# Output projection of a recurrent attention kernel: early weight chunks in 512-column matmuls, the last five in halves

## The chip, the cores and the metric

The kernel runs on one core of one Trainium2 chip (trn2). The metric is the time of one execution on the device in microseconds (us). The kernel before took 1822.86 us, the median of three runs (1820.21, 1822.86 and 1832.62).

A core has five engines that matter here. TensorE does matmuls (PE in the profile, its weight loads are PEld), VectorE (DVE) and ScalarE (ACT) do elementwise work, GpSimd (POOL) and SyncE (SP) mostly issue DMAs. TensorE writes to PSUM, an accumulator memory with banks of 512 float32 columns by 128 partitions; the engines work from SBUF. The engines run side by side and wait for one another by semaphores; on each engine the instructions run in their order.

## The reference, cut to what matters

The output joins two independent parts along the last axis. Part A is a convolution by FFT with gates and is not touched by the change. Part B is a recurrent attention: 64 segments of 32 tokens, each of them with 8 memory rows in front that the segment before has made.

```python
mem = mem0
for s in range(n_seg):                                # 64 segments
    h = concat([mem, x[:, s*32:(s+1)*32]], axis=1)    # 40 rows of 1024
    q, k, v = h @ Wq, h @ Wk, h @ Wv                  # 32 heads of 128 each
    p = softmax(where(mask, q @ k.T * scale, -1e9))
    o = p @ v
    o = einsum('bhte,hed->btd', o, Wo)                # output projection, 4096 -> 1024
    mem = o[:, :8]
    outs.append(o[:, 8:])
```

Segment s+1 needs the memory rows of segment s, so the segments follow one another strictly. Each needs all four weight matrices (Wq, Wk, Wv and Wo, 8 MB each in bfloat16), and they don't all fit into SBUF.

## The kernel before, in words

The program has a front part (part A, and the parts of the keys, queries and values that depend only on x) and then a loop over the 64 segments, unrolled. In the loop the order of the instructions is the order of the program (`manual_schedule`, line 896): each engine gets its instructions as they are written.

The weights are cut into 64 **chunks** of 128 by 2048 elements (512 KB): 16 each of Wk, Wq, Wv and Wo. A chunk of Wo is one pair of heads, `hp` 0 to 15. Most chunks stay in SBUF. Sixteen are "streamed" (`STREAM`, line 29): SP loads them anew in every segment from DRAM into a ring of five buffers (`fetch`, L722 and L720; tiles `wring`). A buffer comes free when the matmuls of its chunk are done (`done`, line 860), and `done` starts the next load. Two of the streamed chunks of Wo, 13 (KEPT_A) and 9 (KEPT_B), are loaded once only, in segment 0. From then on they lie as raw bits in spare columns of PSUM: quarters 0 to 3 of each. From segment 1 on, VectorE copies one quarter at a time into an SBUF tile (`quarter` and `quarter_b`, all through L795) before TensorE uses it. These copies borrow SBUF buffers by their tags ("E", "rot", "QT"), and each has to wait until the earlier content of that buffer has been used.

A segment runs so: keys and queries of two head groups (`Proj`, L938, with accumulators `acc`), transposes, scores, softmax, values, `attend` and `evac_o` (L1007 to L1019), and then the output projection into `yacc`. The projection turns the attention output `OT` (two groups, OT0 and OT1) into 40 rows of 1024. Columns 0 to 511 of the result stand in PSUM partitions 0 to 63 and columns 512 to 1023 in partitions 64 to 127, so each step is a **pair** of matmuls (dh = 0 and 1) that write the two halves of the partitions. `project` (line 1022) does the two pairs of one head, each 256 columns wide: half f = 0 goes into the bank `yacc[0]`, half f = 1 into the bank `yacc[1]`. `out_half` does a chunk's two heads for one half. The order of the chunks is FIRST (0, 1, 2, 3), then 4, then group 1's attention (attend, evac_o, on line 1089), then 5, 6, 7, some quarters, 8, and LAST (10, 15, 11, 12, 14). FIRST and LAST go through the chunks twice, first all halves f = 0 and then all halves f = 1; the others do both halves of a chunk together. In LAST the remaining quarters are put in between (`steps`).

When half f = 0 is complete, ScalarE copies it to the tile Y (L1118). While TensorE does half f = 1, `fill_mem` (L885 on TensorE, L892 on VectorE) turns the memory rows of Y's first half into the operand hT of the next segment. The next segment's first matmuls (keys, k0, four chunks that need only this half) then start while ScalarE copies the second half of Y. After them `fill_mem` handles that second half.

The accumulators `acc` and `yacc` share one pool of two PSUM banks (`ps_acc`, line 780, tag "acc"), eight tiles a segment: k0, q0, k1, q1, pv0, pv1, yacc[0], yacc[1]. A new tile waits until all readers of the bank's earlier tile are done.

Of the kernel before, what the change touches and what calls it, by code (L numbers as in the profile page):

```python
# [10 lines left out]
F32 = mybir.dt.float32  # L11
I32 = mybir.dt.int32
ACT = mybir.ActivationFunctionType
ALU = mybir.AluOpType
# [4 lines left out]
NEG = -1.0e9  # L19


FIRST, LAST = (0, 1, 2, 3), (10, 15, 11, 12, 14)
KEPT_A, KEPT_B = (3, 13, 0), (3, 9, 0)
PART = (3, 4, 0)
O_ORDER = (*FIRST, 4, 5, 6, 7, 9, 13, 8, *LAST)
ORDER = [(0, kc, 0) for kc in (0, 1, 4, 5)] + [(1, kc, 0) for kc in (0, 1)] + [(0, kc, 0) for kc in (2, 3, 6, 7)] + \
    [(1, kc, 0) for kc in range(2, 8)] + [(m, kc, 1) for m in (0, 1) for kc in range(8)] + \
    [(2, kc, g) for g in range(2) for kc in range(8)] + [(3, hp, 0) for hp in O_ORDER]
STREAM = (0, 6, 13, 19, 24, 29, 35, 40, 45, 51, 52, 54, 56, 57, 58, 63)
# [391 lines left out]
def b_kernel(ctx: ExitStack, tc, x, mem0, Wq, Wk, Wv, Wo, outb, n_seg, run_a):  # L421
    nc = tc.nc
# [314 lines left out]
    with c0p:  # L737
# [16 lines left out]
        for g in range(2):  # L754
# [23 lines left out]
    one = ctx.enter_context(tc.tile_pool(name="b_one", bufs=1, side="right", reuse_waits="tile"))  # L778
# [15 lines left out]
    def bits(dst, src):  # L794
        nc.vector.tensor_scalar(out=dst, in0=src, scalar1=0, scalar2=None, op0=ALU.bitwise_or)  # L795

    def like(ap, home):
        return ap.rearrange("p (b x) -> p b x", b=4) if len(home.shape) == 3 else ap

    def quarter_b(q, tag):  # L800
        t = one.tile([128, 256], I32, tag=tag, name="quarter_b")
        w = []
        for home, at in B_homes[q]:
            n = home.shape[1] * (home.shape[2] if len(home.shape) == 3 else 1)
            if home.shape == B_rest[:].shape:
                part = home.bitcast(BF)
            else:
# [32 lines left out]
    def quarter(q, tag):  # L840
        t = one.tile([128, 512], BF, tag=tag, name="quarter")
        bits(t[:].bitcast(I32), OTi[:, q, 160:416])
        return [(o, o + 256, t[:, 256 * dh:256 * dh + 256]) for dh, o in enumerate(quarter_cols(q))]

    def pieces(ch):
        if ch in res:
            return [(0, 2048, res[ch])]
        if now[0] == 0 and ch in at_hand:
            return [(0, 2048, at_hand[ch][0])]
        if ch == PART:  # L850
            return [(0, 512, part[:]), (512, 2048, live[now[0], ch][1][:, 512:2048])]
        return [(0, 2048, live[now[0], ch][1][:])]

    def columns(ps, a, b):
        for lo, hi, w in ps:
            x, y = max(a, lo), min(b, hi)
            if x < y:
                yield x, y, w[:, x - lo:y - lo]

    def done(ch):  # L860
        if now[0] == 0 and ch in at_hand:
            place_late(1, at_hand[ch][1])
        elif ch in streamed and (now[0] == 0 or ch not in kept):
# [32 lines left out]
    with tc.manual_schedule():  # L896
        for _ in range(RING - 2):
            fetch()
        load_x(0)
        Y = one.tile([128, 512], BF, tag="PT", name="Y0")  # L900
        nc.vector.memset(Y[:], 0.0)
        for dh in range(2):
            nc.gpsimd.dma_start(Y[64 * dh:64 * dh + NM, :], mem0[:, dh * 512:(dh + 1) * 512])
        nc.tensor.matmul(SB[:, 0:320], lhsT=ident[:], rhs=P_pad[:].rearrange("p b k -> p (b k)"), start=True, stop=True,
                         skip_group_check=True)
# [7 lines left out]
        for s in range(n_seg):  # L913
# [105 lines left out]
                nc.scalar.copy(OT[:], o_view)  # L1019
                return OT  # L1020

            def project(h, f, w, OT, stop=False):
                k = 40 * (h % 16)
                m = min(64, 640 - k)
                lhsT = OT[:].rearrange("p c i q -> p (c i q)")[:, k:k + m]
                for dh in range(2):
                    o = (h % 2) * 1024 + dh * 512 + f * 256
                    for x, y, r in columns(w, o, o + 256):
                        nc.tensor.matmul(yacc[f][64 * dh:64 * dh + m, x - o:y - o], lhsT=lhsT,  # L1029
                                         rhs=r, start=(h == (0, 2 * FIRST[-1])[f] and x == o), stop=stop,  # L1030
                                         tile_position=(0, 64 * dh))

            def out_half(hp, f, OT, stop=False):
                w = pieces((3, hp, 0))
                for hh in range(2):
                    project(2 * hp + hh, f, w, OT, stop and hh == 1)
                if f == 1:
                    done((3, hp, 0))

            def out_proj(hps, OT):  # L1040
                for hp in hps:
                    for f in range(2):
                        out_half(hp, f, OT)

            def out_quarter(ch, q, w):
                project(2 * ch[1] + q // 2, q % 2, w, OT1)

            if s == 0:
                fill_mem(hT, Y, 0)
            k0 = Proj(0, 0).run(4)  # L1050
# [27 lines left out]
            OT0 = evac_o(0)  # L1078
# [3 lines left out]
                load_x(s + 1)  # L1082
            V1 = pv1.evac()
            yacc = [ps_acc.tile([128, 512], F32, tag="acc", name="yacc") for f in range(2)]
            for f, hps in enumerate((FIRST, FIRST[-1:] + FIRST[:-1])):
                for hp in hps:
                    out_half(hp, f, OT0)
            out_proj((4,), OT0)
            attend(1, PT1, V1)
            OT1 = evac_o(1)  # L1090
            qs = {}
            if s == 0:
                out_proj((5, 6, 7), OT0)
                out_proj((9, 13, 8), OT1)
                steps = {}
            else:
                qs["B", 0], qs["A", 0] = quarter_b(0, "E"), quarter(0, "rot")
                out_proj((5, 6, 7), OT0)
                qs["B", 2] = quarter_b(2, "QT")
                out_quarter(KEPT_B, 0, qs["B", 0])  # L1100
                qs["A", 2] = quarter(2, "E")
                out_quarter(KEPT_A, 0, qs["A", 0])
                qs["A", 1] = quarter(1, "rot")
                out_proj((8,), OT1)
                steps = {(0, 0): [("B", 2), ("B", 1, "QT")], (0, 1): [("A", 2), ("A", 3, "E")],
                         (0, 3): [("A", 1), ("B", 3, "rot")], (1, 0): [("B", 1)], (1, 1): [("A", 3)], (1, 2): [("B", 3)]}
            Y = one.tile([128, 512], BF, tag="PT", name="Y")
            for f, hps in enumerate((LAST, LAST[-1:] + LAST[:-1])):
                for n, hp in enumerate(hps):
                    if f == 1 and n == 3 and not last:  # L1110
                        fill_mem(pend[s + 1][0], Y, 0)
                    out_half(hp, f, OT1, n == 4)
                    for step in steps.get((f, n), ()):
                        if len(step) == 2:
                            out_quarter(KEPT_A if step[0] == "A" else KEPT_B, step[1], qs.pop(step))
                        else:
                            qs[step[:2]] = (quarter if step[0] == "A" else quarter_b)(*step[1:])
                nc.scalar.copy(Y[:, 256 * f:256 * f + 256], yacc[f][:, 0:256])  # L1118
            for dh in range(2):
                nc.gpsimd.dma_start(bass.AP(outb.tensor, outb.offset + SEG * s * 2048 + 512 * dh, [[2048, 32], [1, 512]]),  # L1120
                                    Y[64 * dh + NM:64 * dh + 40, :])
# [71 lines left out]
```

## Time and profile before

| what | value |
|---|---|
| runs, median (lowest to highest) | 1822.86 us (1820.21 to 1832.62) |
| span of the profiled execution, first to last instruction | 1811.8 us |
| the profiled execution's own time | not listed apart from the runs; the median less the span is 11.1 us |
| PE busy | 1701.8 us (94%), 30996 matmuls |
| DVE, ACT, POOL busy | 1010.3, 680.7, 266.7 us (56%, 38%, 15%) |
| second-half copies of Y, start of the first and the last | 475.2 and 1807.5 us |
| the same as time of one segment, mean of 63 | 21.15 us |
| matmuls and weight loads of one segment (1555.54 to 1576.38 us) | 461 and 459 |
| DMA share in the loop | 0.97 to 0.98 in stretches of 100 us from 1000 to 1700 us |

The page of the profile gives busy times and shares of the whole span. The timeline lists instructions in order of time: start, duration, engine, line, operation, output<-inputs, shape and how many were merged into the row, and in brackets the idle time of the engine before it and what ended it. Matmuls are pipelined, so a row's duration overlaps the next row; the distance from start to start is what counts. L1029 is the projection, L938 the keys, queries and values.

### The profile page before, as it was taken

Reading aid. Unit: us, or ns where it says so; the run is one execution under the profiler, and the core shown is the slowest. Engines: PE = TensorE matmul, PEld = TensorE weight load, DVE = VectorE, ACT = ScalarE, POOL = GpSimd, SP = SyncE. Lnnn points to the kernel's source line nnn. Section 1 sums busy time; section 2 is a strip of 40 time slices with the busy share of each in tenths; the row PEclk is TensorE's granted clock in tenths of the full one; section 3 lists DMA queues with packets and bytes.
Section 4 is the critical chain, followed back from the end, with each engine's and each line's share of the span. In section 5 each row is a group of like instructions: output and inputs, shape, how many; then the busy total and the mean of one; then the engine's idle time right before and its main releaser. Section 6 shows DMA issues by size and latency. Waiting matters only on the chain.

```text
span 1811.8 us, 71373 instructions
## 1 busy us (share of the span) xinstructions
PE 1701.8 (94%) x30996; PEld 1000.8 (55%) x31028; DVE 1010.3 (56%) x3391; ACT 680.7 (38%) x1195; POOL 266.7 (15%) x499
## 2 busy tenths in 40 slices
PE   6888996759899999999999999999999999999998
PEld 3443322324566666666666666666666666666665
DVE  9927874201455555555555555555555555555555
ACT  6955651112233333333333333333333333333333
POOL 4003341100111111111111111111111111111111
PEclk9999999889999999999999999999999999999999
DMA  9989889997999999999999999999999999999998
GB/s 340 370 305 305 311 258 320 306 335 210 344 365 361 357 350 360 358 363 353 361 356 358 357 352 360 370 358 360 361 355 362 356 358 366 367 363 356 357 358 300
DMA packets 233070, 623.34 MB, mean 344 GB/s; under 512 B 72802, under 2 KB 72946, under 8 KB 232756
## 3 DMA queue, kind: packets, MB, share of 16 engines
q1 hardware_dynamic: 160948, 550.58, 82.4%
q0 software_dynamic: 17056, 45.13, 7.1%
q10 hardware_dynamic: 54752, 23.07, 4.7%
q8 instruction: 243, 3.98, 0.9%
q14 instruction: 71, 0.58, 0.1%
HBM read 563.63 MB, written 57.67 MB: 343 GB/s over the span
## 4 chain that ended last, share of the span: by engine, by line
PE 77%; DMA 9%; DVE 6%; ACT 4%; issue 3%; ACTq 0%; POOL 0%; SPq 0%; another core or an unknown queue 0%; POOLq 0%; DVEq 0%
PE acc L938 33%; PE yacc L1029 24%; PE kb_ps L622 5%; DMA wring<-WS 4%; PE tps L885 3%; PE tps L957 2%; PE vb_ps L763 2%; ACT OT L1019 2%; DMA REC<-stage 2%; DVE mx L972 1%; DVE E L974 1%; ACT s_sb L247 1%; PE OTp L1007 1%; PE s_ps L245 1%; PE SB L963 1%
## 5 line engine op out<-in xcount | busy, mean ns | idle before, releaser
L1029 PEld LDWEIGHTS <-OT 128*64 128x64 bf16 x8255 | 439.1, 109 | 54.6 <-ACT OT L1019 36.9
L938 PEld LDWEIGHTS <-rec 128*32 128x32 bf16 x12288 | 289.4, 96 | 269.3 <-DVE rec L892 35.2
L947 ACT CAST qkv_sb<-acc 128x512 bf16<-128x512 f32 x384 | 225.1, 586 | 352.2 <-PE acc L938 346.9
L938 PE MATMUL acc<-Wres,rec 128*32 128x512 bf16 x3328 | 240.2, 382 | 2.0 <-issue 1.8
L938 PE MATMUL acc<-wring,rec 128*32 128x512 bf16 x2300 | 229.0, 382 | 8.5 <-DMA wring<-WS 7.3
L1029 PE MATMUL yacc<-Wmore,OT 128*64 128x256 bf16 (+1 forms) x2560 | 220.7, 274 | 0.0
L938 PE MATMUL acc<-Wmid,rec 128*32 128x512 bf16 x3072 | 212.1, 379 | 0.5 <-issue 0.3
L1029 PE MATMUL yacc<-wring,OT 128*64 128x256 bf16 x2448 | 194.9, 273 | 2.7 <-DMA wring<-WS 2.5
L1118 ACT CAST Y<-yacc 128x256 bf16<-128x256 f32 x128 | 47.7, 373 | 269.8 <-DVE quarter_b L795 170.8
L938 PE MATMUL acc<-pw,rec 128*32 128x512 bf16 x1796 | 144.7, 380 | 2.0 <-issue 1.9
L795 DVE TENSOR_SCALAR quarter<-OTp 128x256 int32<-128x256 int32 x252 | 99.9, 418 | 74.3 <-ACT OT L1019 74.3
L1019 ACT CAST OT<-OTp 128x640 bf16<-128x640 f32 x128 | 87.4, 683 | 138.5 <-PE OTp L1011 138.5
L1120 POOL DMA_DIRECT2D out_dram<-Y x128 | 63.9, 503 | 496.3 <-ACT Y L1118 496.0
L892 DVE COPY rec<-tps 128x32 bf16<-128x32 bf16 x128 | 22.4, 175 | 193.6 <-PE tps L885 193.6
L938 PE MATMUL acc<-Wlate,rec 128*32 128x512 bf16 x1536 | 117.3, 379 | 0.1
L1057 DVE COPY KT<-tps 128x512 bf16<-128x512 bf16 x64 | 27.2, 425 | 150.8 <-PE tps L885 150.8
L972 DVE TENSOR_REDUCE mx<-SB 128x8 f32<-128x320 f32 x128 | 63.0, 492 | 78.4 <-PE SB L966 78.4
L880 POOL DMA_DIRECT2D rec<-REC x64 | 36.4, 568 | 453.4 <-PE acc L938 437.9
L977 ACT ACTIVATE E<-E 128x320 f32<-128x320 f32 x128 | 60.1, 469 | 78.3 <-DVE E L974 78.3
L1029 PE MATMUL yacc<-Wlate,OT 128*64 128x256 bf16 x1024 | 79.2, 276 | 6.0 <-issue 0.2
L622 PE MATMUL kb_ps<-XBT,pw 128*128 128x512 bf16 x313 | 81.1, 397 | 2.6 <-DMA pw<-in_B_Wk_dram 1.2
L922 POOL COPY KT<-rec 128x128 bf16<-128x128 bf16 x128 | 38.5, 301 | 253.3 <-PE SB L966 253.3
(224 smaller groups left out, 2627.4 us busy)
## 6 DMA issues: line engine op xcount, KB each, us to landing
wring<-WS SPq DMA_DIRECT2D x831, 512.0 KB, 6.0
wring<-WS SPq DMA_DIRECT2D x64, 384.0 KB, 5.4
rec<-REC POOLq DMA_DIRECT2D x64, 192.0 KB, 5.6
SK<-s_sb SPq DMA_DIRECT2D x16, 512.0 KB, 5.3
SU<-s_sb SPq DMA_DIRECT2D x16, 512.0 KB, 5.6
Kg<-SK SPq DMA_DIRECT2D x32, 256.0 KB, 4.1
Ug<-SU SPq DMA_DIRECT2D x32, 256.0 KB, 5.5
REC<-stage ACTq DMA_DIRECT2D x16, 512.0 KB, 12.9
```

The costliest lines, as they stand in the source:

```text
L622: nc.tensor.matmul(ps[:], lhsT=ws[kc][:, hl * 128:(hl + 1) * 128], rhs=xbt(kc).rearrange("p s t -> p (s t)"), start=(kc == 0), stop=(kc == 7))
L795: nc.vector.tensor_scalar(out=dst, in0=src, scalar1=0, scalar2=None, op0=ALU.bitwise_or)
L885: nc.tensor.matmul(dst[e:e + 32, :], lhsT=src[:, e:e + 32], rhs=ident[:], start=True, stop=True, is_transpose=True, tile_position=(0, e))
L922: nc.gpsimd.tensor_copy(KT[:, :, :, 32:40], KBs[:, 128 * g:128 * g + 128].rearrange("p (c i t) -> p i c t", c=4, i=4))
L938: nc.tensor.matmul(self.acc[32 * c:32 * c + 32, :], lhsT=hT[:, ch[1], :], rhs=w[:, 512 * c:512 * c + 512], start=(ch == chs[0]), stop=(ch ...
L947: nc.scalar.copy(sb[:], self.acc[:])
L972: nc.vector.tensor_reduce(out=mx[:], in_=S, op=ALU.max, axis=AX.X)
L977: nc.scalar.activation(E[:], E[:], ACT.Exp, scale=scale)
L1019: nc.scalar.copy(OT[:], o_view)
L1029: nc.tensor.matmul(yacc[f][64 * dh:64 * dh + m, x - o:y - o], lhsT=lhsT, rhs=r, start=(h == (0, 2 * FIRST[-1])[f] and x == o), stop=stop, ...
L1118: nc.scalar.copy(Y[:, 256 * f:256 * f + 256], yacc[f][:, 0:256])
L1120: nc.gpsimd.dma_start(bass.AP(outb.tensor, outb.offset + SEG * s * 2048 + 512 * dh, [[2048, 32], [1, 512]]), Y[64 * dh + NM:64 * dh + 40, :])
```

## The change

Instead of two banks by half, most of the projection goes into one bank. `project` takes a range of columns and a bank. The chunks EARLY (0 to 4), 5, 6, 7 and 8 (in segment 0 also 9 and 13) are done by `out_full`: one matmul of 512 columns in place of two of 256, all into `yacc[0]`. Only LAST stays in halves. Its half f = 0 is accumulated in the other bank, `yacc[1]`, together with quarters 2 of the kept chunks. For that half, ScalarE copies the sum of the early chunks, columns 0 to 255 of `yacc[0]`, to a float32 tile y0; after half f = 0, VectorE adds y0 and the bank `yacc[1]` into Y, where ScalarE made a copy before. Half f = 1 of LAST goes on in `yacc[0]`, columns 256 to 511, and ScalarE copies it to Y as before. Since y0 takes the buffer "rot", the copies and uses of quarters 1, 2 and 3 change their places.

```diff
-FIRST, LAST = (0, 1, 2, 3), (10, 15, 11, 12, 14)
+EARLY, LAST = (0, 1, 2, 3, 4), (10, 15, 11, 12, 14)
...
-            def project(h, f, w, OT, stop=False):
+            def project(h, a, b, w, OT, bank, at, start=False, stop=False):
...
-                    o = (h % 2) * 1024 + dh * 512 + f * 256
-                    for x, y, r in columns(w, o, o + 256):
-                        nc.tensor.matmul(yacc[f][64 * dh:64 * dh + m, x - o:y - o], lhsT=lhsT,
-                                         rhs=r, start=(h == (0, 2 * FIRST[-1])[f] and x == o), stop=stop,
+                    o = (h % 2) * 1024 + dh * 512 + a
+                    for x, y, r in columns(w, o, o + b - a):
+                        nc.tensor.matmul(bank[64 * dh:64 * dh + m, at + x - o:at + y - o], lhsT=lhsT, rhs=r,
+                                         start=start and x == o, stop=stop, skip_group_check=True,
                                          tile_position=(0, 64 * dh))
...
+            def out_full(hps, OT):
+                for hp in hps:
+                    w = pieces((3, hp, 0))
+                    for hh in range(2):
+                        project(2 * hp + hh, 0, 512, w, OT, yacc[0], 0, start=hp == 0 and hh == 0)
+                    done((3, hp, 0))
+            def out_half(hp, f, first, stop):
+                w = pieces((3, hp, 0))
+                for hh in range(2):
+                    project(2 * hp + hh, 256 * f, 256 * f + 256, w, OT1, yacc[1 - f], 256 * f,
+                            start=first and f == 0 and hh == 0, stop=stop and hh == 1)
+                if f == 1:
+                    done((3, hp, 0))
...
+            def out_quarter(ch, q, in_last=False):
+                f = q % 2
+                project(2 * ch[1] + q // 2, 256 * f, 256 * f + 256, qs.pop((ch, q)), OT1,
+                        yacc[1] if in_last and f == 0 else yacc[0], 256 * f)
+            def bring(ch, q, tag):
+                qs[ch, q] = (quarter if ch == KEPT_A else quarter_b)(q, tag)
...
-                steps = {(0, 0): [("B", 2), ("B", 1, "QT")], (0, 1): [("A", 2), ("A", 3, "E")],
-                         (0, 3): [("A", 1), ("B", 3, "rot")], (1, 0): [("B", 1)], (1, 1): [("A", 3)], (1, 2): [("B", 3)]}
+                bring(KEPT_B, 0, "E")
+                bring(KEPT_A, 0, "rot")
+                out_full((5, 6, 7), OT0)
+                bring(KEPT_B, 2, "QT")
+                out_quarter(KEPT_B, 0)
+                bring(KEPT_A, 2, "E")
+                out_quarter(KEPT_A, 0)
+                out_full((8,), OT1)
+                steps = {(0, 1): [(KEPT_B, 2), (KEPT_B, 1, "QT")], (0, 3): [(KEPT_A, 2)],
+                         (1, 0): [(KEPT_A, 1, "E"), (KEPT_B, 1), (KEPT_B, 3, "rot"), (KEPT_A, 3, "QT")],
+                         (1, 2): [(KEPT_A, 1)], (1, 3): [(KEPT_B, 3), (KEPT_A, 3)]}
             Y = one.tile([128, 512], BF, tag="PT", name="Y")
+            y0 = one.tile([128, 256], F32, tag="rot", name="y0")
+            nc.scalar.copy(y0[:], yacc[0][:, 0:256])
...
-                nc.scalar.copy(Y[:, 256 * f:256 * f + 256], yacc[f][:, 0:256])
+                if f == 0:
+                    nc.vector.tensor_tensor(out=Y[:, 0:256], in0=yacc[1][:, 0:256], in1=y0[:], op=ALU.add)
+                else:
+                    nc.scalar.copy(Y[:, 256:512], yacc[0][:, 256:512])
```

In `steps` a key (f, n) says after which chunk of LAST something happens; an entry with a tag is a copy by VectorE (`bring`), one without is a use by TensorE (`out_quarter`). `pieces`, `columns`, `done`, `quarter` and `quarter_b` are unchanged.

More of the change, by code (lines that the diff above doesn't have):

```diff
@@ L19 @@
 NEG = -1.0e9
-FIRST, LAST = (0, 1, 2, 3), (10, 15, 11, 12, 14)
+EARLY, LAST = (0, 1, 2, 3, 4), (10, 15, 11, 12, 14)
 KEPT_A, KEPT_B = (3, 13, 0), (3, 9, 0)
 PART = (3, 4, 0)
-O_ORDER = (*FIRST, 4, 5, 6, 7, 9, 13, 8, *LAST)
+O_ORDER = (*EARLY, 5, 6, 7, 9, 13, 8, *LAST)
 ORDER = [(0, kc, 0) for kc in (0, 1, 4, 5)] + [(1, kc, 0) for kc in (0, 1)] + [(0, kc, 0) for kc in (2, 3, 6, 7)] + \
@@ L1026, in project @@
                 for dh in range(2):
-                    o = (h % 2) * 1024 + dh * 512 + f * 256
-                    for x, y, r in columns(w, o, o + 256):
-                        nc.tensor.matmul(yacc[f][64 * dh:64 * dh + m, x - o:y - o], lhsT=lhsT,
-                                         rhs=r, start=(h == (0, 2 * FIRST[-1])[f] and x == o), stop=stop,
+                    o = (h % 2) * 1024 + dh * 512 + a
+                    for x, y, r in columns(w, o, o + b - a):
+                        nc.tensor.matmul(bank[64 * dh:64 * dh + m, at + x - o:at + y - o], lhsT=lhsT, rhs=r,
+                                         start=start and x == o, stop=stop, skip_group_check=True,
                                          tile_position=(0, 64 * dh))
-            def out_half(hp, f, OT, stop=False):
+            def out_full(hps, OT):
[5 more added lines that the diff above has]
+            def out_half(hp, f, first, stop):
                 w = pieces((3, hp, 0))
                 for hh in range(2):
-                    project(2 * hp + hh, f, w, OT, stop and hh == 1)
+                    project(2 * hp + hh, 256 * f, 256 * f + 256, w, OT1, yacc[1 - f], 256 * f,
+                            start=first and f == 0 and hh == 0, stop=stop and hh == 1)
                 if f == 1:
                     done((3, hp, 0))
[L1040 to L1046, printed above, removed]
+            def out_quarter(ch, q, in_last=False):
[4 more added lines that the diff above has]
+                qs[ch, q] = (quarter if ch == KEPT_A else quarter_b)(q, tag)
             if s == 0:
@@ L1084, in b_kernel @@
             yacc = [ps_acc.tile([128, 512], F32, tag="acc", name="yacc") for f in range(2)]
[L1085 to L1088, printed above, removed]
+            qs = {}
+            out_full(EARLY, OT0)
             attend(1, PT1, V1)
             OT1 = evac_o(1)
-            qs = {}
             if s == 0:
-                out_proj((5, 6, 7), OT0)
-                out_proj((9, 13, 8), OT1)
+                out_full((5, 6, 7), OT0)
+                out_full((9, 13, 8), OT1)
                 steps = {}
             else:
[L1097 to L1104, printed above, removed]
-                steps = {(0, 0): [("B", 2), ("B", 1, "QT")], (0, 1): [("A", 2), ("A", 3, "E")],
-                         (0, 3): [("A", 1), ("B", 3, "rot")], (1, 0): [("B", 1)], (1, 1): [("A", 3)], (1, 2): [("B", 3)]}
+                bring(KEPT_B, 0, "E")
+                bring(KEPT_A, 0, "rot")
+                out_full((5, 6, 7), OT0)
+                bring(KEPT_B, 2, "QT")
[6 more added lines that the diff above has]
+                         (1, 2): [(KEPT_A, 1)], (1, 3): [(KEPT_B, 3), (KEPT_A, 3)]}
             Y = one.tile([128, 512], BF, tag="PT", name="Y")
+            y0 = one.tile([128, 256], F32, tag="rot", name="y0")
+            nc.scalar.copy(y0[:], yacc[0][:, 0:256])
             for f, hps in enumerate((LAST, LAST[-1:] + LAST[:-1])):
@@ L1111, in b_kernel @@
                         fill_mem(pend[s + 1][0], Y, 0)
-                    out_half(hp, f, OT1, n == 4)
+                    out_half(hp, f, n == 0, n == 4)
                     for step in steps.get((f, n), ()):
                         if len(step) == 2:
-                            out_quarter(KEPT_A if step[0] == "A" else KEPT_B, step[1], qs.pop(step))
+                            out_quarter(*step, in_last=True)
                         else:
-                            qs[step[:2]] = (quarter if step[0] == "A" else quarter_b)(*step[1:])
-                nc.scalar.copy(Y[:, 256 * f:256 * f + 256], yacc[f][:, 0:256])
+                            bring(*step)
+                if f == 0:
+                    nc.vector.tensor_tensor(out=Y[:, 0:256], in0=yacc[1][:, 0:256], in1=y0[:], op=ALU.add)
+                else:
+                    nc.scalar.copy(Y[:, 256:512], yacc[0][:, 256:512])
             for dh in range(2):
```

## The prediction

> **What bounds the kernel.** I read the page first: PE is busy 94% of the span, and in the slices of the segment loop it is full. The next question was whether DMA stands beside it, so I asked for busy times by stretches, each from one second-half copy of Y to the next, that is one segment. Two of them:
>
> ```profile
> 1555.54:1576.38 20.84, 20.73 (x461) 13.17 (x459) 11.94 (x45) 7.53 (x15) 2.70 (x6) 1.00 1.00 376
> 1638.90:1660.87 21.97, 21.07 (x457) 13.07 (x453) 11.91 (x45) 7.64 (x14) 2.70 (x6) 1.00 0.94 342
> ```
>
> Columns: length, then busy time of PE, PEld, DVE, ACT and POOL, granted clock, DMA share, GB/s. The shortest segments all take 20.84 us and PE is busy in 20.73 of it: that is TensorE's own floor. The mean is 21.15 us, (1807.5 - 475.2) / 63, so 0.31 us a segment or 19.5 us in all lies above it. The clock is 1.00 in both, so it isn't that. Who waits, over the loop (totals, times, longest):
>
> ```profile
> PEld L938 <- issue: 16.3, 36, 1.1
> PEld L957 <- issue: 3.2, 8, 0.4
> PEld L963 <- issue: 1.6, 3, 0.8
> PEld L1029 <- issue: 1.4, 5, 0.5
> PE acc L938 <- DMA wring<-WS: 2.0, 6, 0.5
> ```
>
> "Issue" is a wait for nothing that the profile shows. These four rows make 22.5 us, about the excess; weight loads from DRAM only 2.0. So what counts is TensorE's own chain through a segment. The part that the change touches, in the timeline of one segment:
>
> ```profile
> 1698.37 0.42 DVE L795 TENSOR_SCALAR quarter<-OTp 128x256 int32<-128x256 int32 x1 [1.23 <-ACT OT L1019]
> ...
> 1698.91 0.28 PE L1029 MATMUL yacc<-quarter,OT 128*64 128x256 bf16 x2
> ...
> 1699.02 0.60 PE L1029 MATMUL yacc<-wring,OT 128*64 128x256 bf16 x8
> 1699.35 0.75 DVE L795 TENSOR_SCALAR quarter<-OTp 128x256 int32<-128x256 int32 x2
> 1699.46 0.38 PE L1029 MATMUL yacc<-Wmore,OT 128*64 128x256 bf16 x4
> ...
> 1700.66 0.60 PE L1029 MATMUL yacc<-wring,OT 128*64 128x256 bf16 x8
> ...
> 1701.08 0.37 ACT L1118 CAST Y<-yacc 128x256 bf16<-128x256 f32 x1 [2.75 <-DVE quarter_b L795]
> ...
> 1702.74 0.40 PE L938 MATMUL acc<-wring,rec 128*32 128x512 bf16 x4
> 1702.85 0.37 ACT L1118 CAST Y<-yacc 128x256 bf16<-128x256 f32 x1 [1.40 <-PE yacc L1029]
> ```
>
> TensorE never stops here: eight matmuls of 256 columns, four pairs, take 0.435 us (1699.02 to 1699.46), a pair 0.109. The next segment's k0 starts at 1702.74, before the second copy of Y does (1702.85). The first copy begins 0.31 after the start of the last pair that it needs (1700.77); I call that 0.32 below for any engine that waits for TensorE.
>
> **Part 1, 512 columns.** Nine chunks a segment (0 to 8) go from four pairs of 256 to two of 512. A chunk took 0.435. The nearest row of 512 columns is L938, whose groups of four side by side take 0.217 (12 matmuls from 1305.81 to 1306.46):
>
> ```profile
> 1305.81 0.82 PE L938 MATMUL acc<-Wmid,rec 128*32 128x512 bf16 x12
> 1306.46 0.39 PE L938 MATMUL acc<-wring,rec 128*32 128x512 bf16 x4
> ```
>
> Two such take 0.433. TensorE streams the same columns either way, so the saving is 0 to 0.01 a chunk; with 0.004 it is 9 x 0.004 x 64 = 2.3 us. 36 matmuls and 36 weight loads of 461 and 459 go. The loads lay under the matmuls (PEld 13.17 of 20.84), so they save nothing by themselves. The Trainium skill (TensorE: Matmul & The Clock Gate, Back-to-back issue gap) says that in a stream of weight loads and matmuls both set the pace, with 81 ns a matmul at 128 columns and 131 at 512. An estimate from it, 98 ns at 256 columns and two matmuls side by side, would save 4 x 98 - 2 x 131 = 130 ns a chunk, 75 us in all.
>
> **Part 2, fewer instructions to fetch.** The page has a queue of instruction transfers, 243 of 16 KB in 3.98 MB, one per 256 or so of TensorE's 62024 instructions. I take the issue waits for waits on these, since the profile shows nothing else for them. The change takes 72 of 920 instructions a segment, 8%. But it thins out L1029, which has 1.4 us of these waits; the 21 others fall on lines whose instructions stay. I take -1 us, bounds 0 and -22.5. The Trainium skill (Runtime: NRT & Kernel Launch, Instruction fetch mechanics) says that TensorE's program is fetched in blocks of 256 instructions and that this is mostly hidden; by that this part is worth nothing, and the trace agrees on the size of the blocks but shows waits up to 1.1 us.
>
> **Part 3, y0 and the add.** The copy y0 (128x256 out of PSUM, 0.37 by the L1118 row) runs on ScalarE, which between OT1 and the second copy of Y has only the first copy, now gone; nothing waits behind it. It is ready at about 1700.0 (chunk 8's last pair starts at 1699.24, plus 0.1 for its greater width, 0.32 and 0.37), and the add wants it at 1700.97. It costs nothing. The add takes the place of the first copy on VectorE. No such add is in the trace. Above and below it in size:
>
> ```profile
> L974 DVE TENSOR_TENSOR E<-SB,mx x2: 491/492/492, 1709.6 to 1714.1; 128x320 f32<-128x320 f32 x2
> L985 DVE TENSOR_TENSOR P_pad<-E,ssum x1: 284/284/284, 1711.5 to 1711.5; 128x128 bf16<-128x128 f32 x1
> ```
>
> 320 columns take 0.49, 128 take 0.28, so 256 about 0.42 (bounds 0.28 and 0.49). Y's first half is ready 0.05 later than before; `fill_mem` needs it a microsecond later.
>
> **Part 4, the quarters.** VectorE now has, in order: B1, the add, A1, B3, A3. Before, all of these copies stood ahead of the end of half f = 0, A1 as the second in the row of 1699.35; now A1 is queued behind the add. I count from A0's matmul at 1698.91, which stays (its copy ends at 1698.79). TensorE: A0 0.109, chunk 8 0.433, 10 and 15 0.218 each, B2 0.109, 11 and 12 0.218 each, A2 0.109, the first pair of 14 0.109: its last pair of half f = 0 starts at 1700.65 and ends its turn at 1700.76. Then 14, B1, 10 and 15 take 0.763, and TensorE is at A1 at 1701.52. VectorE: B1 waits for B2's matmul at 1699.89 and is read by 1700.7; the add starts 1700.65 + 0.32 = 1700.97; the next copy starts about 0.08 before the one ahead ends (the two in the row of 1699.35 take 0.75, one alone 0.42), so A1's starts at 1701.30 and ends at 1701.72; TensorE can use it 0.05 later, 1701.77. **A wait of 0.25 us**, new in every segment but the first, and queued behind it is everything that TensorE does. Bounds: with the add at 0.28 it is 0.11, with 0.49 and 0.12 from VectorE to TensorE (1698.79 to 1698.91 for A0, a case with no wait) 0.39. B3 and A3 follow by 1702.25; TensorE, now later, gets to them at 1702.5 and 1702.6. `fill_mem`'s copy to hT is also behind them, at about 1702.5, and k0 needs it not before 1702.9. 63 x 0.25 = **15.8 us**, bounds 7 and 25.
>
> **Part 5, loads.** Chunk 3's ring buffer is now released after four whole chunks (8 halves) instead of 5 halves, 0.65 us later, and its load carries k0's first chunk. SP issues it later by that; but loads take 6.0 us to land and two others are ahead in the queue, so it goes on being the queue that decides. Nothing, at most 0.1 a segment; a longer segment leaves DMA more room (it was at 0.98), which I count as -0.5 us in all.
>
> **Sum.** -2.3 - 1 + 15.8 - 0.5 = +12 us. The profiled execution's span of 1811.8 becomes 1824; the median of the runs lies 11.1 above the span, and 1822.9 + 12 = 1835.
>
> **Rivals.** *A, k0 waits for Y's second half.* `yacc[0]` was done first, now it is done last. If k0's accumulator takes the bank of the older tile, `yacc[0]`, it can't start until ScalarE has copied its columns 256 to 511: by the rows above 1702.85 + 0.37 + 0.05 = 1703.27 instead of 1702.74, +0.53 x 63 = 33 us on top, 1868. For it: two banks taken in turn would do just this. Against it: in the program of before, the pool of six PSUM buffers of the second stage of part A gives a new tile the buffer that was released first, not the oldest; here that is `yacc[1]`, free since the add. The trace fits both, as `yacc[0]` was then the oldest and the first released. 12%.
>
> *B, the instruction supply.* Not slower: if the fetch waits depend on where the 256-instruction blocks end, a segment of 850 instructions instead of 920 shifts them, and 13 of the 22.5 us gone pay for part 4. With 20 gone it is 1816. For it: the waits sit at changing places of the segment. Against: the crowded lines stay as they are. 13%.
>
> *C, no wait for A1*, if VectorE's add and copy take 0.25 less than I sum, which no row has: 1835 - 16 = 1819. 12%.
>
> *D, weight loads set the pace* of the 256-column pairs, and half as many free TensorE. Then a pair of 512 would have to run faster than the 0.217 of L938, which loads four times for each group; no row has that. The skill's rule under part 1 would make it 1835 - 75 = 1760. 2%.
>
> My forecast has 60%, 1% is left. Its own range is 1824 to 1847 by the bounds of part 4 and some 3 us of the runs' spread. With B and C the range goes down to 1812; up to 1852 leaves A out. About 1% (18 us) is what a measurement of this kernel can tell from no change, as the runs spread over 12 us: faster than 1804.6 needs D, or B and C together, 7%; slower than 1841 is A and the upper part of mine, 28%; between them 65%.
>
> **What would show it.** After: PE some 425 a segment; L1029 rows of 512 columns at 0.216 a pair; a new wait of TensorE on quarter L795 before A1, 63 times, about 0.25 each, 16 us in total; an add of 0.42; k0 starting ahead of the second copy of Y (A: after it, with a wait on ACT of some 0.5); issue waits near 21 us (B: a few). I'd be wrong if the add's row is far from 0.42, or if k0 waits.

## The result, and the profile after

| what | before | after |
|---|---|---|
| runs, median (lowest to highest) | 1822.71 us (1813.22 to 1832.62, 10 runs) | 1836.68 us (1830.21 to 1839.76, 10 runs) |
| ratio | | 1.0076, 95% interval 1.0055 to 1.0098 |
| span of the profiled execution | 1811.8 us | 1833.0 us |
| its own time | about 1813.6 us (span + 1.8, inferred) | 1834.8 us |
| segment, mean of 63 | 21.15 us | 21.42 us |
| shortest segment that recurs | 20.84 us | 21.14 us |

The kernel became slower by 14.0 us, 0.8%, against a forecast of +12 us and 1835. Wherever both are listed the time lies 1.7 to 1.9 us above the span (2.2 with the add twice), so the profiled execution of before took about 1813.6 us, at the low end of its runs (an inference: its own time is not listed). The difference of the two spans, 21.2 us, therefore overstates the change; medians and the floor of a segment are the figures to compare.

First the busy times in two segments of after, as before from one second-half copy of Y to the next (length, busy time of PE, PEld, DVE, ACT and POOL, granted clock, DMA share, GB/s):

```profile
630.81:651.96 21.15, 20.88 (x425) 11.27 (x425) 12.45 (x46) 7.53 (x15) 2.69 (x6) 1.00 0.97 355
651.96:673.10 21.14, 20.98 (x425) 11.34 (x423) 12.36 (x46) 7.52 (x15) 2.69 (x6) 1.00 0.99 373
```

TensorE has 425 matmuls and not 461, and the floor is 0.30 us higher. Its busy time is no guide to the wait: a row's end is modelled and laps over what follows. In the timeline of after, around the halves, the wait shows from start to start:

```profile
649.31 0.60 PE L1029 MATMUL yacc<-wring,OT 128*64 128x256 bf16 x8
...
649.80 0.42 DVE L1127 TENSOR_TENSOR Y<-yacc,y 128x256 bf16<-128x256 f32 x1 [0.35 <-PE yacc L1029]
649.85 0.60 PE L1029 MATMUL yacc<-Wmore,OT 128*64 128x256 bf16 x8
650.15 0.41 DVE L795 TENSOR_SCALAR quarter<-OTp 128x256 int32<-128x256 int32 x1
...
650.61 0.30 PE L1029 MATMUL yacc<-quarter,OT 128*64 128x256 bf16 x2 [0.16 <-DVE quarter L795]
650.62 0.11 PEld L1029 LDWEIGHTS <-OT 128*64 128x64 bf16 x1 [0.32 <-issue]
651.53 0.39 PE L1029 MATMUL yacc<-pw,OT 128*64 128x256 bf16 x4
651.85 0.40 PE L938 MATMUL acc<-wring,rec 128*32 128x512 bf16 x4
651.96 0.37 ACT L1129 CAST Y<-yacc 128x256 bf16<-128x256 f32 x1 [3.16 <-PE yacc L1029]
```

The eight matmuls of 649.85 are four pairs, over at 650.29 by their starts (4 x 0.109). A1's pair starts at 650.61, when the copy of 650.15 has ended: TensorE stood for 0.32 us. The bracket at A1 says 0.16 only, since it counts from the modelled end of the row ahead; the weight load's row behind it has the whole 0.32, but under "issue". At the seam, where the projection of one segment ends and k0 of the next one begins, k0 (651.85) still starts ahead of the second copy of Y (651.96).

The waits of after (total, times, longest), TensorE's weight loads first:

```profile
PEld L938 <- issue: 25.7, 85, 0.9
PEld L1029 <- issue: 21.9, 66, 0.9
```

```profile
PE yacc L1029 <- DVE quarter L795: 9.5, 61, 0.2
PE acc L938 <- DMA wring<-WS: 3.2, 8, 0.8
```

The wait for A1 is new, 61 times; the row L1029 of the weight loads, 21.9 us in 66, is mostly that same wait seen in full. Over all segments, A1 starts 0.433 us after the start of the pair ahead in place of 0.109: 0.324 x 63 = **20.4 us**. That is more than the 14.0 us that the whole change costs, so something gives back, and the experiments have to say what.

### The profile page after: what moved, and what is told of

Its sections match the earlier page's. It is cut to its first block, busy times and chain, and to the rows that moved or that the text cites. A ratio compares the mean times of both kernels' runs of the same rounds, so it can differ in the third digit from the quotient of the medians.

```text
span 1833.0 us, 66690 instructions
## 1 busy us (share of the span) xinstructions
PE 1712.2 (93%) x28684; PEld 879.1 (48%) x28716; DVE 1036.4 (57%) x3455; ACT 680.1 (37%) x1195; POOL 265.8 (14%) x499
## 4 chain that ended last, share of the span: by engine, by line
PE 75%; DMA 10%; DVE 8%; ACT 4%; issue 3%; POOL 0%; ACTq 0%; SPq 0%; DVEq 0%; another core or an unknown queue 0%; POOLq 0%
PE acc L938 32%; PE yacc L1029 22%; PE kb_ps L622 5%; DMA wring<-WS 5%; PE tps L885 3%; PE tps L957 2%; PE vb_ps L763 2%; DMA REC<-stage 2%; ACT OT L1019 2%; ACT s_sb L247 1%; DVE Y L1127 1%; DVE mx L972 1%; DVE E L974 1%; DVE quarter L795 1%; PE s_ps L245 1%
## 5 line engine op out<-in xcount | busy, mean ns | idle before, releaser
L938 PEld LDWEIGHTS <-rec 128*32 128x32 bf16 x12288 | 288.4, 96 | 267.0 <-issue 34.8
L1029 PEld LDWEIGHTS <-OT 128*64 128x64 bf16 x5943 | 317.6, 109 | 179.0 <-ACT OT L1019 36.0
L938 PE MATMUL acc<-Wres,rec 128*32 128x512 bf16 x3328 | 240.1, 382 | 0.4 <-issue 0.3
L938 PE MATMUL acc<-wring,rec 128*32 128x512 bf16 x2300 | 227.9, 382 | 10.9 <-DMA wring<-WS 9.2
L938 PE MATMUL acc<-Wmid,rec 128*32 128x512 bf16 x3072 | 211.5, 379 | 0.1
L1029 PE MATMUL yacc<-Wmore,OT 128*64 128x512 bf16 (+3 forms) x1792 | 194.9, 321 | 0.0
L1029 PE MATMUL yacc<-wring,OT 128*64 128x512 bf16 (+1 forms) x1480 | 183.0, 343 | 3.9 <-DMA wring<-WS 3.9
L795 DVE TENSOR_SCALAR quarter<-OTp 128x256 int32<-128x256 int32 x252 | 104.8, 416 | 72.6 <-ACT OT L1019 72.6
L938 PE MATMUL acc<-pw,rec 128*32 128x512 bf16 x1796 | 143.5, 380 | 0.2 <-issue 0.2
L938 PE MATMUL acc<-Wlate,rec 128*32 128x512 bf16 x1536 | 116.3, 379 | 0.0
L1129 ACT CAST Y<-yacc 128x256 bf16<-128x256 f32 x64 | 23.8, 372 | 203.4 <-PE yacc L1029 203.4
L1029 PE MATMUL yacc<-quarter,OT 128*64 128x256 bf16 x504 | 71.4, 275 | 9.9 <-DVE quarter L795 9.5
```

The lines of the kernel that those rows point to most:

```text
L938: nc.tensor.matmul(self.acc[32 * c:32 * c + 32, :], lhsT=hT[:, ch[1], :], rhs=w[:, 512 * c:512 * c + 512], start=(ch == chs[0]), stop=(ch ...
L1029: nc.tensor.matmul(bank[64 * dh:64 * dh + m, at + x - o:at + y - o], lhsT=lhsT, rhs=r, start=start and x == o, stop=stop, skip_group_check ...
```

## The experiments

Theory Q (queue) is the prediction's part 4: what costs is A1's copy, queued behind the add. Its rivals are the supply of instructions (parts 1 and 2, rival B), the load of chunk 3 (part 5), and rival A, k0 waiting for Y's second half. All kernels below but the last are edits of after. "Against before" is the difference of the medians, with before run again beside each kernel. Each ratio's interval is 0.14 to 0.25% either way, so a single difference of two changed kernels is uncertain by some 4 to 6 us.

| kernel | median (runs) | before beside it | ratio, 95% interval | against before | floor of a segment |
|---|---|---|---|---|---|
| after | 1836.68 (10) | 1822.71 | 1.0076, 1.0055 to 1.0098 | +14.0 | 21.14 |
| A1 later | 1823.99 (10) | 1823.01 | 1.0003, 0.9987 to 1.0019 | +1.0 | 20.83 |
| chunk 3 second | 1830.33 (7) | 1823.01 | 1.0045, 1.0028 to 1.0061 | +7.3 | 21.14 |
| both | 1815.16 (9) | 1822.55 | 0.9957, 0.9938 to 0.9976 | -7.4 | 20.83 |
| both, 256 columns | 1823.27 (12) | 1822.55 | 1.0001, 0.9987 to 1.0015 | +0.7 | 20.87 |
| after, 256 columns | 1842.76 (4) | 1823.01 | 1.0111, 1.0090 to 1.0132 | +19.8 | 21.19 |
| y0 by VectorE | 1833.99 (6) | 1822.55 | 1.0063, 1.0039 to 1.0087 | +11.4 | 21.08 |
| add twice | 1859.22 (4) | 1823.01 | 1.0204, 1.0179 to 1.0228 | +36.2 | 21.60 |
| bank read late | 1859.54 (4) | 1822.55 | 1.0204, 1.0181 to 1.0228 | +37.0 | 21.67 |
| before, chunk 3 late | 1829.94 (12) | 1821.62 | 1.0048, 1.0027 to 1.0069 | +8.3 | 20.85 |

### A1 used later

```diff
-                         (1, 2): [(KEPT_A, 1)], (1, 3): [(KEPT_B, 3), (KEPT_A, 3)]}
+                         (1, 3): [(KEPT_A, 1), (KEPT_B, 3), (KEPT_A, 3)]}
```

TensorE now does `fill_mem`'s transposes (0.23 us) and chunk 11's two pairs (0.22 us) ahead of A1, some 0.45 us of work, so that the copy is there in time.

> The changed kernel with one quarter moved: A1 is used by TensorE after chunk 11 instead of after chunk 15, some 0.56 us later in the segment; VectorE's order (add, A1, B3, A3) stays. Theory Q (TensorE waits because A1's copy stands behind the add in VectorE's queue): the wait of 0.32 us a segment goes, 63 x 0.32 = 20 us, about 1816 us, faster than both kernels. Rival W (the wait only hides another cost of the change, such as a late load or the next copy being late): another wait takes its place and the time stays within 5 us of 1837. Half way, about 1826, would say that A3 or the memory rows are late next.

Measured 1823.99, 12.7 below after by the medians and 13.0 by the differences against before. A segment of it:

```profile
733.17:754.00 20.83, 20.72 (x425) 11.20 (x425) 12.26 (x46) 7.54 (x15) 2.68 (x6) 1.00 1.00 366
```

The floor is down to 20.83, by 0.31, which is the whole wait: TensorE's wait for A1's copy makes the new floor. (That the add ahead of it in VectorE's queue is what makes the copy late is tested below, with the add twice.) But 63 x 0.31 is 20 us, where 1816 was expected, and 13 arrived. One wait grew:

```profile
PE acc L938 <- DMA wring<-WS: 10.2, 23, 0.9
```

TensorE now waits 23 times for a chunk from DRAM at the beginning of a segment, 10.2 us in place of 3.2. Most of that (7.3 us) stands at the seam, at k0's first chunk, the one that takes chunk 3's ring buffer: part 5, which I had costed at nothing.

### Chunk 3 second

```diff
-            out_full(EARLY, OT0)
+            out_full((0, 3, 1, 2, 4), OT0)
```

The ring buffer of chunk 3 is released after two whole chunks instead of four; chunks 1 and 2, which are not streamed, come behind it, and nothing else moves.

> The changed kernel with chunk 3 done second instead of fourth (order 0, 3, 1, 2, 4), so that its ring buffer comes free 0.86 us earlier for k0's first chunk. If the later release costs what the seam shows (12 of 62 segments in which k0 starts over 0.25 us after the last pair, against 3 before; 3.3 us in all against 0.8): those fall to 3 or 4 and the time by 2 to 3 us, about 1834. If the queue of loads decides, as predicted: no change, 1837, and still about 12 late starts.

Measured 1830.33, 6.7 less than after by the differences against before. Waits:

```profile
PE yacc L1029 <- DVE quarter L795: 9.0, 58, 0.2
PE acc L938 <- DMA wring<-WS: 1.9, 4, 0.6
```

The wait for A1 stays as it was and the one for the load shrinks to 1.9 us; of the 12 late starts of k0 one is left. The gain was expected to be 2 to 3 us, and the row fell by 1.3 us only, less than the time did, so by this run alone the price would be weak; the next two runs repeat the step in other surroundings.

### Both, and the late chunk alone in the kernel before

Both edits together:

> Both moves together: A1 used after chunk 11, and chunk 3 done second. Theory Q, with loads as what is late next: with A1 late alone 1824, 25 of 62 segments then started k0 late, 8.4 us in all; these go (1 late start was left when chunk 3 alone was moved), so about 1816, 6 to 7 us below the kernel before. If loads only move their lateness to another chunk: about 1824, and the profile shows waits on wring at other lines.

Measured **1815.16**, 7.4 us faster than before and 21.4 faster than after; it beats both kernels. The floor and the wait for the load:

```profile
733.29:754.12 20.83, 20.72 (x425) 11.20 (x425) 12.27 (x46) 7.53 (x15) 2.68 (x6) 1.00 1.01 381
```

```profile
PE acc L938 <- DMA wring<-WS: 2.8, 5, 0.9
```

The floor is that of "A1 later", so the 8.4 us between them are no work of TensorE: most of them are the late load (10.2 us of waits against 2.8). The other way round, in the kernel before, with chunk 3 last of the first four in both halves:

```diff
-            for f, hps in enumerate((FIRST, FIRST[-1:] + FIRST[:-1])):
+            for f, hps in enumerate((FIRST, FIRST)):
...
-                                         rhs=r, start=(h == (0, 2 * FIRST[-1])[f] and x == o), stop=stop,
+                                         rhs=r, start=(h == 0 and x == o), stop=stop,
```

> The kernel before with one part of the change alone: its second pass over FIRST goes 0, 1, 2, 3 instead of 3, 0, 1, 2, so that chunk 3 is done after 8 halves instead of 5, 0.65 us later, as in the changed kernel; the same matmuls, copies and adds otherwise. If the late release by itself costs what moving chunk 3 forward gave back (1836.7 to 1830.3 in the changed kernel, 1824.0 to 1815.2 with A1 late): 6 to 9 us more, about 1830, and k0 starts late in 10 to 25 of 62 segments instead of 3. If the queue of loads decides, as predicted: no change, 1822.6.

Measured 1829.94, +8.3 us. The floor does not move (20.85), the load's wait does:

```profile
541.08:561.93 20.85, 20.74 (x461) 13.14 (x461) 11.93 (x45) 7.53 (x15) 2.69 (x6) 1.00 1.01 371
```

```profile
PE acc L938 <- DMA wring<-WS: 11.2, 20, 1.5
```

From 2.0 us in 6 waits to 11.2 us in 20, and the time by about as much. Three pairs of kernels that differ in nothing but the place of chunk 3 give 6.7, 8.4 and 8.3 us.

The landings in the traces show how. The load of k0's first chunk is issued 6.54 us ahead of k0 in before and 5.89 with chunk 3 late (medians of 63 segments), and two or three earlier loads are still under way then, as the prediction said. But the load does not land at the same time in spite of that: it has landed 0.89 us ahead of k0 in before and 0.36 with chunk 3 late. Of the 0.65 us by which it was issued later, 0.53 came through. Likewise the lead is 0.78 in after and 1.04 with chunk 3 second, 0.34 with A1 later and 0.75 with both; the release moved by some 0.86 in these two pairs.

### 256 columns again

The same bank and the same order, but two matmuls of 256 columns where the change has one of 512:

```diff
-                        project(2 * hp + hh, 0, 512, w, OT, yacc[0], 0, start=hp == 0 and hh == 0)
+                        for f in range(2):
+                            project(2 * hp + hh, 256 * f, 256 * f + 256, w, OT, yacc[0], 256 * f,
+                                    start=hp == 0 and hh == 0 and f == 0)
```

> The changed kernel with the early chunks again in two matmuls of 256 columns, but all in the one bank; order, add and quarters stay. Theory Q, with the width worth 0.004 to 0.005 us a chunk and the instruction supply nearly nothing: +3 us, about 1840. Rival S (the 72 instructions fewer a segment shorten the waits for instructions: within the L938 lines they fell from 10.5 to 4.6 us between the two profiles): these waits come back, +9 us, about 1846, and the profile shows them at 10 us or more. If the wide matmuls cost something: below 1837.

Measured 1842.76, between the two that were expected: by the differences against before the width is worth 5.8 us in the kernel after. The same edit in the kernel with both moves, where A1's wait and the late load are gone:

> The same two moves with the early chunks in matmuls of 256 columns. If the width is worth what the streams show (0.3 us in all): as its twin with 512. Theory S (fewer instructions shorten the waits for instructions): 6 us more than its twin, as between 1842.8 and 1836.7, about 1822, and more issue waits at L938.

Measured 1823.27, 8.1 us above its twin. A segment of each, the one on after first:

```profile
606.83:628.02 21.19, 20.92 (x461) 13.18 (x460) 12.35 (x46) 7.53 (x14) 2.68 (x6) 1.00 0.98 357
```

```profile
710.99:731.86 20.87, 20.76 (x461) 13.09 (x461) 12.27 (x46) 7.54 (x15) 2.69 (x6) 1.00 1.00 369
```

The floors are 0.04 to 0.05 above those with 512 columns, which makes 2.5 to 3.2 us of the 6 to 8. The rest, some 3 to 6 us, is clear of the uncertainty only in the second pair, and not by much. It would fit the 8% of instructions that TensorE no longer has to be sent: after's page lists 225 transfers where before's had 243.

```profile
q8 instruction: 225, 3.69, 0.8%
```

That is an argument and was not shown. The issue waits of L938 bear on it, but have to be read with care. They make 16.3 us in 36 in before and 25.7 in 85 in after, which looks like more; yet 62 of the 85 (15.1 us) stand at the seam, ahead of k0's first weight load, where before's view names VectorE's `rec` in its place. The row of `rec`, first in before, then in after:

```profile
PEld L938 <- DVE rec L892: 34.9, 126, 0.6
PEld L938 <- DVE rec L892: 21.8, 64, 0.3
```

Without the seam they are 10.6 us in 23 in after, against 16.3 in 36 in before and 18.2 in 35 with 256 columns again; in the other pair 14.6 in 25 with both moves and 18.0 in 37 with 256 columns. So there are fewer of these waits with 512 columns in both pairs, as theory S has it. But the starts of the matmuls follow only once. Intervals of more than 0.26 us between matmuls within L938, less the usual 0.216 and without those put down to a load, make 7.7 us in before, 2.7 in after and 7.2 in after with 256 columns, but 7.4 in either kernel of the second pair, and the two executions profiled there took the same time (1817.89 and 1818.05 us). The cause of these 3 to 6 us stays open.

### y0 by VectorE

In after the add starts 0.388 us after the start of the last pair that it needs; I had taken 0.318. It waits for two other engines, TensorE's sum and ScalarE's y0. VectorE's queue has a semaphore row ahead of it that holds the wait for TensorE; the add itself is left with the wait for y0, which is long ready. The line of the add (lowest, median and highest ns, then first to last):

```profile
L1127 DVEq EVENT_SEMAPHORE  x64: 21/21/21, 477.2 to 1826.9; - x64
L1127 DVE TENSOR_TENSOR Y<-yacc,y x64: 423/425/425, 477.3 to 1826.9; 128x256 bf16<-128x256 f32 x64
```

The row of 21 ns starts 0.066 us ahead of the add in every segment, that is 0.32 after the pair.

If VectorE makes y0 itself, early on, the add need not wait for ScalarE:

```diff
-            nc.scalar.copy(y0[:], yacc[0][:, 0:256])
+            nc.vector.tensor_copy(y0[:], yacc[0][:, 0:256])
```

> The changed kernel with the copy y0 on VectorE instead of ScalarE, so that the add waits on TensorE alone. The add began 0.388 us after the pair that it needs, the other copies 0.318; if the 0.07 is its second semaphore, it begins at 0.32, the wait before A1 is 0.25 as predicted in place of 0.32, and the time falls by 4 us to about 1832. If the 0.07 belongs to the add itself (two inputs): no change, 1837.

```profile
584.39 0.60 PE L1029 MATMUL yacc<-wring,OT 128*64 128x256 bf16 x8
584.82 0.42 DVE L1127 TENSOR_TENSOR Y<-yacc,y 128x256 bf16<-128x256 f32 x1 [0.28 <-PE yacc L1029]
...
585.63 0.11 PEld L1029 LDWEIGHTS <-OT 128*64 128x64 bf16 x1 [0.25 <-issue]
```

```profile
565.89:586.97 21.08, 20.88 (x425) 11.31 (x425) 12.69 (x47) 7.16 (x13) 2.68 (x6) 1.00 0.99 364
```

The last pair of the half starts 0.109 after the row, at 584.50, and the add 0.32 later; the bracket has 0.28 where it had 0.35, and the wait before A1 is 0.25. The floor fell by 0.065 us, 4.1 us over 63 segments. The semaphore row is still there, but it stands some 0.75 us ahead of the add and waits for something earlier; the wait for TensorE has moved into the add itself. The first copies of Y on ScalarE in before have semaphore rows too, 3 us and more ahead of them; they wait for TensorE themselves and start 0.31 to 0.32 after the pair. So it is not the number of engines to wait for that costs the 0.07 us: they came when the wait that ends last stood in a row of its own. Of the time, 1833.99, only 2.6 us can be seen, within its uncertainty.

### The add twice

The line of the add is there a second time, with the same output:

```diff
                     nc.vector.tensor_tensor(out=Y[:, 0:256], in0=yacc[1][:, 0:256], in1=y0[:], op=ALU.add)
+                    nc.vector.tensor_tensor(out=Y[:, 0:256], in0=yacc[1][:, 0:256], in1=y0[:], op=ALU.add)
```

> The changed kernel with the add done twice, the second one the same again. Theory Q: A1's copy comes 0.34 us later, and so does everything of TensorE after it; 63 x 0.34 = 21 us more, about 1858, the wait before A1 grows from 0.32 to 0.66. Rival W (VectorE is busy 57% of the time and has room; the wait has another cause): within 3 us of 1837.

```profile
672.53 0.42 DVE L1127 TENSOR_TENSOR Y<-yacc,y 128x256 bf16<-128x256 f32 x1 [0.35 <-PE yacc L1029]
672.99 0.42 DVE L1128 TENSOR_TENSOR Y<-yacc,y 128x256 bf16<-128x256 f32 x1
673.33 0.41 DVE L795 TENSOR_SCALAR quarter<-OTp 128x256 int32<-128x256 int32 x1
```

```profile
631.94:653.54 21.60, 20.88 (x425) 11.28 (x425) 12.78 (x47) 7.53 (x14) 2.69 (x6) 1.00 0.98 351
```

The second add starts 0.46 after the first, later than the first one's end, where A1's copy starts 0.34 after the add; I had expected 0.34 for both. (Both adds write the same tile; that this is what keeps them apart was not tried.) The floor rose by the same 0.46, to 21.60: what VectorE does ahead of A1's copy goes straight into TensorE's chain. That is 0.46 x 63 = 29 us, and 22.2 was measured; that 1859.22 came out next to the 1858 expected is two errors that offset each other.

### The bank read late

Rival A did not come about in after: at the seam k0 starts 0.208 after the pair ahead of it, as in before (0.206). To see its price, the bank that k0 took is given a last reader behind the second copy of Y:

```diff
                     nc.scalar.copy(Y[:, 256:512], yacc[0][:, 256:512])
+                    late_read = two.tile([128, 8], F32, tag="mx", name="late_read")
+                    nc.scalar.copy(late_read[:], yacc[1][:, 0:8])
```

What is read is used nowhere.

> The changed kernel with one more read of yacc[1] on ScalarE (8 columns, after the second copy of Y), so that yacc[0] is released first and k0 gets its bank. Rival A's price: k0 waits for the second copy of Y, +0.53 us x 63 = 33 us, about 1870. If k0 had to wait for nothing: 1837.

```profile
566.34 0.39 PE L1029 MATMUL yacc<-pw,OT 128*64 128x256 bf16 x4
566.77 0.37 ACT L1129 CAST Y<-yacc 128x256 bf16<-128x256 f32 x1 [3.16 <-PE yacc L1029]
567.04 0.17 ACT L1131 COPY late_read<-yacc 128x8 f32<-128x8 f32 x1
567.19 0.40 PE L938 MATMUL acc<-wring,rec 128*32 128x512 bf16 x4 [0.46 <-ACT Y L1129]
```

```profile
PE acc L938 <- ACT Y L1129: 27.8, 60, 0.5
```

```profile
545.10:566.77 21.67, 20.94 (x421) 11.40 (x421) 12.35 (x46) 7.60 (x15) 2.69 (x6) 1.00 0.99 349
```

k0 now starts behind the second copy of Y (566.77 + 0.37 + 0.05 = 567.19), and its wait names that copy, L1129. The small read of `yacc[1]` is not yet over then, so k0 took the bank `yacc[0]`, again the one released first. The seam is 0.74 in place of 0.208, 0.53 more, just the price that the prediction gave rival A, and the floor 21.67 is 0.53 above after's. Over 63 segments this makes 33 us; 23.0 more than after were measured (1859.54, where 1870 was expected).

## Why the prediction was right, and where it was not

**The whole.** 1836.68 against 1835, inside the range and within 1%, by the mechanism of part 4. But the sum came within 2 us of the measured difference by errors that offset one another, and that closeness is luck. The runs give a chain in which one thing changes at a time, as differences against before: the new banks, halves and add without A1's wait, late chunk or width +0.7; with 512 columns -7.4, so the width -8.1; with A1's wait +7.3 (chunk 3 second), so the wait +14.7; with the late chunk +14.0, so that +6.7. Each step has the 4 to 6 us of uncertainty of a difference; A1's and the chunk's were measured in a second surrounding too (13.0; 8.4 and 8.3).

**Parts 1 and 2** (512 columns, instructions): forecast -2.3 and -1, measured together -5.8 and -8.1. They look mis-sized, though with an uncertainty of 4 to 6 us the first value doesn't exclude -3.3 and the second just does. The part of the floor is as forecast, 0.04 to 0.05 us a segment for nine chunks; the other 3 to 6 us are what stays open above. The Trainium skill (TensorE: Matmul & The Clock Gate, Back-to-back issue gap) would have given -75 us by the estimate made in the prediction; the measured -5.8 and -8.1 speak against it for these pairs, as do the starts, 0.109 apart at 256 columns and 0.216 at 512. The Trainium skill (Runtime: NRT & Kernel Launch, Instruction fetch mechanics) calls the fetch mostly hidden; the 3 to 6 us neither prove nor refute that.

**Part 3** (y0 and the add): right in its sizes. The add takes 0.425 (forecast 0.42), and y0 is ready a microsecond ahead of it. But with y0 on another engine the add has a second wait, and by that it starts 0.07 later; this is counted under part 4.

**Part 4** (A1): the mechanism was right, in the place and for the reason given. Its size was 0.324 and not 0.25 us a segment: the term mis-sized is the start of the add, "0.32 for any engine that waits for TensorE", which is 0.39 for the add, whose wait for TensorE stands in a row of its own. On the other side, 20.4 us at the floor brought 13.0 and 14.7 in time, since other waits shrank when it came (which ones, the traces show only in part). The forecast of 15.8 for the time was thus near by two errors.

**Part 5** (the load of chunk 3): this is the step that failed. It argued that a release 0.65 us later changes nothing, as two other loads are ahead in the queue anyway. Two or three were, but they did not absorb the delay: in before with chunk 3 late the load landed 0.53 us nearer to k0, and in 20 segments k0 started late, against 3. With a DMA share of 0.97 to 1.01 in the segments shown there was not enough slack. Three pairs of kernels put the price at 6.7 to 8.4 us, where I had nothing, and -0.5 for the DMA's extra room.

**"The median lies 11.1 above the span"** was wrong as a reading. The time is 1.8 above its own span; the other 9.3 were the distance of one execution at the low end of the runs from their median. It did no harm to the sum, which adds a difference to a median, but the excess over the floor read from that profile, 19.5 us, is that of one execution, by the spans one of the fastest.

**Rivals.** A did not occur, because the pool gave k0 the bank that was released first, as the row against it had said; its price was exact at the floor, and in time 23.0 of the 33 us arrived. C did not occur; "A1 later" shows what it would have given, 1824, and the prediction had 1819. B came in at most in part (3 to 6 us of its 13), with fewer issue waits at L938 as its sign and its cause not shown. D, with weight loads as the pace, is excluded by the starts of the pairs.

## What to carry to other kernels

When work moves from one engine to another, list what stands behind it in the new engine's queue: the add cost nothing by itself, but the copy behind it stopped TensorE in 63 segments, and using that copy's result some 0.45 us later in TensorE's order took the whole wait out of the floor, and 13.0 and 14.7 us out of the time. When a loop's order changes, look at when each buffer of the load ring is released; at a DMA share near 1, a release 0.65 to 0.86 us later cost about half as much as the new stall. Count a stall at the floor, but expect only part of it in the time (some two thirds to three quarters here, each stall with 4 to 6 us of uncertainty) as long as other waits can shrink behind it.

## What the runs showed of the hardware that was not expected

An add whose wait for TensorE stood in a semaphore row of its own, 21 ns long and directly ahead of it, began 0.07 us later after TensorE's last pair (0.388) than instructions that hold this wait themselves (0.32), the others' semaphore rows having gone by earlier.

A stall put into TensorE's chain is not paid in full. The mean segment of one profile lies above the floor by 0.28 us in after, 0.21 with the add twice and 0.14 with the bank read late: in these three, the longer TensorE stands at a fixed place, the less it waits elsewhere. (They are single executions; after with 256 columns has the same stall as after and 0.43.) By the medians, 22.2 of 29 us and 23.0 of 33 were measured; and where the wait for A1 was taken out, 13.0 and 14.7 of 20 were gained. With the late chunk the wait for its load took up part of that (3.2 us to 10.2). With chunk 3 second it did not (1.9 to 2.8), and which wait came back there was not found.
